# Down projection of a spectral layer with an FFN: each 512-column matmul issued as two of 256 columns

## The chip, the cores and the metric

The kernel runs on one core of one Trainium2 chip. The metric is the device time of one execution in microseconds, lower is better. Before the change it is 2627.49 us, the median of 3 runs (2627.15 to 2628.44).

On the core, TensorE multiplies matrices: a matmul streams the columns of its moving operand (`rhs`) past 128x128 weights (`lhsT`) and writes or adds into a bank of PSUM, 512 fp32 columns wide. The weights get there by a load that stands in front of each matmul as an instruction of its own. VectorE, ScalarE and GpSimd do the elementwise work, and SyncE issues the transfers.

## The reference

```
X = rfft(x, axis=1)                                  # x: 8 x 3008 x 256
Yr = X.real @ w_r - X.imag @ w_i + b_r
Yi = X.real @ w_i + X.imag @ w_r + b_i
Y = shrink(Yr, 0.01) + 1j * shrink(Yi, 0.01)         # sign(y) * max(|y| - 0.01, 0)
y = irfft(Y, n=3008, axis=1).reshape(24064, 256)
h = y @ w_in                                         # 256 -> 2048
g = h * clip(h + 3, 0, 6) / 6
out = g @ w_out                                      # 2048 -> 256, "down projection"
```

## The kernel before

**Precision.** A value is split into a high and a low part of type float32r, and a product is the sum of three matmuls: low x high, high x low, high x high (`product`, L137, and the two-letter keys of `STEPS` for the down projection).

**Stages.** The two Fourier transforms are small matmuls of 64, 47 and 128 points, with a trip through DRAM between them (L308, L394, L471, L523; their results go into the banks `ps_a`, and `pb` for the first sequence). For one sequence after the other they leave columns of `y`, 256 features by 512 tokens, in tiles `raw`. 47 such chunks of tokens go through the FFN in 8 steps each, so there are 376 units, each of 256 hidden features and 512 tokens.

**A unit.** The up projection of a unit is one Strassen-Winograd step: 7 blocks of 3 matmuls of 256 columns (weights `w_in`, moving operand `yb`, both hi and lo) into three banks: `pb` (two buffers; blocks 1, 6, 7 and 4 add up in it, and it is read by ScalarE between them, L585 and L619), `pc` (block 5, and then block 3 on top of it; VectorE reads it after each, L590) and `pd` (block 2; read by VectorE, L590). `pc` and `pd` have one buffer each. The sums stand in `h`. The gate is then four instructions of 1024 columns: ScalarE `r = relu(h + 3)` (L626), VectorE `r = min(r, 6) * h` (L628), ScalarE `gs` high (a cast, L130), VectorE `gs` low (L131).

**The down projection of a unit** (`down`, L649) is 12 matmuls of 512 columns in four steps of three: for two slices `u` of the hidden features and two halves `dh` of the 256 outputs, w_out low x g high, w_out high x g high, and w_out high x g low. They add up in two banks `po0` and `po1` over the 8 units of a chunk; after the last, ScalarE and VectorE copy the banks to `ot` (times 1/6), which is stored. That makes 376 x 12 = 4512 matmuls of this line.

**What sets the order.** The code lays a unit's phases one behind another (phase A of unit i, down step 0 of unit i - 3, phase C of unit i - 1, and so on), and hangs the pieces of the Fourier stages of the next sequences into slots between them. A planner then orders the instructions of each engine anew: it plays the program on a timeline with prices of its own, and picks at each point, by readiness and place in the code, what goes next (`TileContext(nc, schedule_with_timeline_sim=True)`). So a matmul that is priced or cut in another way can move every instruction behind it, on every engine.

Of the kernel before, what the change touches and what calls it, by code (L numbers as in the profile page):

```python
# [21 lines left out]
B, S, D, FF = 8, 3008, 256, 2048  # L22
# [3 lines left out]
P = 128  # L26
# [7 lines left out]
H = T // 2  # L34
# [66 lines left out]
def spectral_ffn(ctx: ExitStack, tc: tile.TileContext, x, w_r, w_i, bias, w_in, w_out, f47, f64, g64, sgn, out):  # L101
    nc = tc.nc
# [11 lines left out]
    def space(shape, dt, name, tag=None):  # L114
        tag = tag or name
        return sb.tile(shape, dt, name=name, tag=tag, bufs=depth.get(tag, 1))
# [41 lines left out]
    nf = NFT // 2  # L158
# [403 lines left out]
    def prepare(c):  # L562
        y = raw.pop(c)
        b11, b12, b21, b22 = y[:, 0, :H], y[:, 0, H:], y[:, 1, :H], y[:, 1, H:]
        s = space([P, 4, H], F32, "T")
        for to, p, q in ((0, b12, b11), (1, b22, s[:, 0]), (2, b22, b12), (3, b21, s[:, 1])):
            (nc.gpsimd if c else nc.vector).tensor_tensor(out=s[:, to], in0=p, in1=q, op=ALU.subtract)
        yield
        for n, src in ((2, b21), (1, b11), (6, s[:, 1]), (7, s[:, 2]), (5, s[:, 0]), (4, s[:, 3]), (3, b22)):
            t = space([P, 2, H], F32R, "yb")  # L570
            split(t[:, 0], t[:, 1], src, nc.gpsimd if c else nc.vector)
            yb[c, n] = (t[:, 0], t[:, 1])
            yield

    units = [(c, f) for c in range(NC) for f in range(nf)]
    hs, ps_of, keep, gs, pos = {}, {}, {}, {}, {}
# [63 lines left out]
    def down(i, step):  # L640

        c, f = units[i]
        g = gs[i]
        for u, dh, which, low in STEPS[step]:
            if f == 0 and step < 2 and u == 0 and which == "l":
                pos[dh] = ps_o.tile([P, 512], F32, name=f"po{dh}")
            ft = 2 * f + u
            w = wout_s["hl".index(which)]
            nc.tensor.matmul(  # L649
                out=pos[dh],  # L650
                lhsT=w[:, ft * D + dh * P : ft * D + (dh + 1) * P],
                rhs=g[:, low, u],
                start=f == 0 and u == 0 and which == "l",
                stop=f == nf - 1 and u == 1 and low == 1,
            )
            if f == nf - 1 and u == 1 and low == 1:
                ot = space([P, T], F32, "ot")
                if dh:
                    nc.vector.tensor_scalar(out=ot, in0=pos[dh], scalar1=1.0 / 6.0, scalar2=None, op0=ALU.mult)
                else:  # L660
                    nc.scalar.mul(out=ot, in_=pos[dh], mul=1.0 / 6.0)
                nc.sync.dma_start(out=out[dh * P : (dh + 1) * P, c * T : (c + 1) * T], in_=ot)
# [42 lines left out]
    for c in range(1, NC):  # L705
        g = prepare(c)
# [24 lines left out]
    for i in range(n + 3):  # L731
        for kind, f in ((in_band, i), (out_band, i - 3)):
            while 0 <= f < nf and (kind, f) not in ready:
                turn(LATE)
        if i < n:
            phase_a(i)
        gated(i - 2)
        fill(4 * i)
        if 0 <= i - 3 < n:
            down(i - 3, 0)  # L740
        if 0 <= i - 1 < n:
            phase_c(i - 1)
        fill(4 * i + 1)
        if 0 <= i - 3 < n:
            down(i - 3, 1)
        if i < n:
            phase_b(i)
        fill(4 * i + 2)
        if 0 <= i - 3 < n:
            down(i - 3, 2)  # L750
        if 0 <= i - 1 < n:
            phase_d(i - 1)
            gates[i - 1] = gate(i - 1)
            gated(i - 1)
        fill(4 * i + 3)
        if 0 <= i - 3 < n:
            down(i - 3, 3)
            gs.pop(i - 3)
# [47 lines left out]
```

## Time and profile before

| | us | share of the span |
|---|---|---|
| median of 3 runs | 2627.49 | |
| span of the profiled execution | 2628.8 | 100% |
| TensorE matmuls busy | 2554.0 | 97% |
| TensorE weight loads busy | 2278.1 | 87% |
| VectorE busy | 1967.7 | 75% |
| ScalarE busy | 1816.7 | 69% |
| GpSimd busy | 762.9 | 29% |

The profiled execution's own time is its span, 2628.8 us, which is 0.4 us above the slowest of the three timed runs. Matmuls are pipelined, and their ends are modelled: a 512-column matmul is shown with 396 ns, though the next one starts 233 ns after it. So the busy time of a matmul is not its price. Its price is the distance from its start to the next start where nothing waits, and rows that merge several issues give it (duration by number). In the listings, PE is the matmul, PEld the weight load, DVE is VectorE, ACT ScalarE, POOL GpSimd, SP SyncE.

### The profile page before, as it was taken

To read this page: it belongs to the slowest core of one execution; us is meant where nothing else is said; L and a number is where in the kernel's file an instruction comes from. 1 tells how busy PE (TensorE), PEld (TensorE's weight loads), DVE (VectorE), ACT (ScalarE), POOL (GpSimd) and SP (SyncE) were. 2 spreads that over 40 slices of the span, in tenths; PEclk is the share of its full clock that TensorE was granted. 3 is DMA by queue.
4 is the path that set the end of the run, shared out by engine and by line. 5 is a ranking of instruction groups with operands and counts; after the bars stand their busy time and mean duration, and the time that the engine had idled before them with its cause. 6 is when DMAs were issued, how large, how long until landed. Compare 5 with 4: busy or idle time off the path is not lost.

```text
span 2628.8 us, 44438 instructions
## 1 busy us (share of the span) xinstructions
PE 2554.0 (97%) x16392; PEld 2278.1 (87%) x16392; DVE 1967.7 (75%) x3195; ACT 1816.7 (69%) x3578; POOL 762.9 (29%) x726
## 2 busy tenths in 40 slices
PE   5789999999999999999999999999999999999999
PEld 4568989988898988998898888898989889888887
DVE  7777877777777777777778777787777777666766
ACT  5467776767677676676766677766776766776666
POOL 3223333333323332333314243233321121131310
PEclk8999999999999999999999999999999999999999
DMA  8643422232123212322223222222222111110000
GB/s 245 204 127 91 121 83 79 82 89 69 56 85 90 76 58 64 86 86 82 62 66 91 75 65 74 74 81 80 66 76 64 44 60 50 40 31 25 12 17 17
DMA packets 150081, 199.97 MB, mean 76 GB/s; under 512 B 16847, under 2 KB 103943, under 8 KB 149863
## 3 DMA queue, kind: packets, MB, share of 16 engines
q1 hardware_dynamic: 149863, 197.13, 25.7%
q8 instruction: 129, 2.11, 0.4%
q14 instruction: 89, 0.73, 0.1%
HBM read 97.45 MB, written 74.97 MB: 66 GB/s over the span
## 4 chain that ended last, share of the span: by engine, by line
PE 83%; DVE 6%; ACT 5%; DMA 4%; issue 1%; SPq 0%; POOL 0%; ACTq 0%; DVEq 0%
PE po L649 37%; PE pb L137 17%; PE ps_a L137 10%; PE pc L137 9%; PE pd L137 4%; PE ps_a L523 3%; PE ps_a L394 2%; ACT r L626 2%; DVE r L628 1%; ACT gs L130 1%; DMA scr<-a 1%; DMA xin<-in_x 1%; DVE gs L131 1%; DVE h L590 1%; DMA zt<-tc 1%
## 5 line engine op out<-in xcount | busy, mean ns | idle before, releaser
L649 PE MATMUL po<-gs,w_out_hi 128*128 128x512 f32 x3008 | 1008.5, 396 | 0.0
L628 DVE SCALAR_TENSOR_TENSOR r<-r,h 128x1024 f32<-128x1024 f32 x376 | 485.2, 1290 | 253.0 <-ACT r L626 250.9
L649 PEld LDWEIGHTS po<-gs,w_out_hi 128*128 128x128 f32 x3008 | 540.6, 188 | 83.7
L649 PE MATMUL po<-gs,w_out_lo 128*128 128x512 f32 x1504 | 602.9, 401 | 5.3 <-ACT gs L130 3.2
L137 PE MATMUL pb<-yb,w_in_hi 128*128 128x256 f32 x3008 | 570.1, 279 | 0.0
L626 ACT ACTIVATE r<-h,three 128x1024 f32<-128x1024 f32 x376 | 435.6, 1158 | 193.8 <-DVE h L590 191.1
L131 DVE TENSOR_TENSOR gs<-r,gs 128x1024 fp32r<-128x1024 f32 x376 | 481.9, 1282 | 75.6 <-ACT gs L130 74.1
L137 PEld LDWEIGHTS pb<-yb,w_in_hi 128*128 128x128 f32 x3008 | 459.1, 188 | 18.2
L130 ACT CAST gs<-r 128x1024 fp32r<-128x1024 f32 x376 | 396.7, 1055 | 97.3 <-DVE r L628 94.5
L590 DVE TENSOR_TENSOR h<-pc,u 128x256 f32<-128x256 f32 x752 | 315.3, 419 | 183.7 <-PE pc L137 168.4
L131 POOL TENSOR_TENSOR yb<-T,yb 128x256 fp32r<-128x256 f32 x184 | 176.7, 966 | 908.5 <-ACT yb L130 905.3
L137 PE MATMUL pb<-yb,w_in_lo 128*128 128x256 f32 x1504 | 430.5, 287 | 3.8 <-ACT p L585 0.9
L585 ACT COPY u<-pb 128x256 f32<-128x256 f32 x752 | 279.4, 374 | 112.6 <-PE pb L137 93.8
L649 PEld LDWEIGHTS po<-gs,w_out_lo 128*128 128x128 f32 x1504 | 282.7, 188 | 63.8 <-ACT gs L130 14.3
L137 PEld LDWEIGHTS pb<-yb,w_in_lo 128*128 128x128 f32 x1504 | 282.6, 188 | 28.2 <-ACT h L619 4.0
L137 PE MATMUL pc<-yb,w_in_hi 128*128 128x256 f32 x1504 | 296.8, 279 | 0.0
L137 PEld LDWEIGHTS pc<-yb,w_in_hi 128*128 128x128 f32 x1504 | 229.8, 188 | 11.7
L137 PE MATMUL pc<-yb,w_in_lo 128*128 128x256 f32 x752 | 217.7, 289 | 2.0 <-DVE h L590 1.7
L585 ACT COPY p<-pb 128x256 f32<-128x256 f32 x376 | 140.3, 374 | 71.6 <-PE pb L137 70.5
L619 ACT COPY h<-pb 128x256 f32<-128x256 f32 x376 | 141.2, 376 | 53.0 <-PE pb L137 51.7
L590 DVE TENSOR_TENSOR h<-pd,p 128x256 f32<-128x256 f32 x376 | 157.0, 418 | 19.8 <-ACT p L585 13.5
L137 PEld LDWEIGHTS pc<-yb,w_in_lo 128*128 128x128 f32 x752 | 141.6, 188 | 16.4 <-DVE h L590 3.9
(139 smaller groups left out, 3873.7 us busy)
## 6 DMA issues: line engine op xcount, KB each, us to landing
bt<-scr SPq DMA_DIRECT2D x96, 256.0 KB, 3.0
scr<-pt SPq DMA_DIRECT2D x96, 256.0 KB, 2.3
zt<-tc SPq DMA_DIRECT2D x376, 64.0 KB, 2.0
out<-ot SPq DMA_DIRECT2D x94, 256.0 KB, 2.3
scr<-a SPq DMA_DIRECT2D x96, 240.0 KB, 2.6
qt<-scr SPq DMA_DIRECT2D x96, 240.0 KB, 3.5
xin<-in_x SPq DMA_DIRECT2D x42, 480.0 KB, 4.6
f<-in_f SPq DMA_DIRECT2D x96, 128.0 KB, 2.7
```

The source lines that it names most:

```text
L130: nc.scalar.copy(out=hi, in_=src)
L131: (on or nc.vector).tensor_tensor(out=lo, in0=src, in1=hi.bitcast(F32), op=ALU.subtract)
L137: nc.tensor.matmul(out=ps, lhsT=a, rhs=b, start=start and n == 0, stop=stop and n == len(todo) - 1, skip_group_check=more,)
L394: nc.tensor.matmul(out=psv[:, dh, :, u, :], lhsT=data[:, u, dh * P : (dh + 1) * P], rhs=f[:, u, :], start=True, stop=True,)
L523: nc.tensor.matmul(out=ps[:, cs * w + g * rows : cs * w + (g + 1) * rows], lhsT=qt[:rows, cs, g, dh * P : (dh + 1) * P], rhs=f47_s[2][:row ...
L585: nc.scalar.copy(out=t, in_=ps)
L590: nc.vector.tensor_tensor(out=to, in0=ps, in1=keep.pop((i, n)), op=ALU.add)
L619: nc.scalar.copy(out=hs[i][:, 1, :H], in_=pb)
L626: nc.scalar.activation(out=r, in_=h, func=AF.Relu, bias=three, scale=1.0)
L628: nc.vector.scalar_tensor_tensor(out=r, in0=r, scalar=6.0, in1=h, op0=ALU.min, op1=ALU.mult)
L649: nc.tensor.matmul(out=pos[dh], lhsT=w[:, ft * D + dh * P : ft * D + (dh + 1) * P], rhs=g[:, low, u], start=f == 0 and u == 0 and which == ...
```

## The change

Each matmul of the down projection is issued as two: the same weights, the first and the second 256 columns of the moving operand, into the first and the second half of the same bank. Nothing else in the code changes; `H` is 256.

```
-            nc.tensor.matmul(
-                out=pos[dh],
-                lhsT=w[:, ft * D + dh * P : ft * D + (dh + 1) * P],
-                rhs=g[:, low, u],
-                start=f == 0 and u == 0 and which == "l",
-                stop=f == nf - 1 and u == 1 and low == 1,
-            )
+            for half in range(2):
+                cols = slice(half * H, (half + 1) * H)
+                nc.tensor.matmul(
+                    out=pos[dh][:, cols],
+                    lhsT=w[:, ft * D + dh * P : ft * D + (dh + 1) * P],
+                    rhs=g[:, low, u, cols],
+                    start=f == 0 and u == 0 and which == "l",
+                    stop=f == nf - 1 and u == 1 and low == 1,
+                    skip_group_check=True,
+                )
```

The planner deals with 4512 more matmuls, and the order changes on all engines from the first down projection on. Two places on TensorE show how. The first is the bank `pc` of the 64th unit: its block 5, what stands behind it, and its block 3, which must wait until VectorE has read block 5. Before (`pc_6694`):

```order
L137 MATMUL pc_6694<-yb_5834,w_in_lo_79 128x256 [waits DVE_49]
L137 MATMUL pc_6694<-yb_5834,w_in_hi_78 128x256 x2
L137 MATMUL pb_6666<-yb_6439,w_in_lo_79 128x256 [waits Activation_49]
L137 MATMUL pb_6666<-yb_6439,w_in_hi_78 128x256 [waits Pool_49]
L137 MATMUL pb_6666<-yb_6439,w_in_hi_78 128x256
L137 MATMUL pb_6772<-yb_6373,w_in_lo_79 128x256 [waits Activation_49]
L137 MATMUL pb_6772<-yb_6373,w_in_hi_78 128x256 x2
L137 MATMUL pc_6694<-yb_5933,w_in_lo_79 128x256 [waits DVE_49]
L137 MATMUL pc_6694<-yb_5933,w_in_hi_78 128x256 x2
```

And now (`pc_7429` is the same unit's bank), from the last two matmuls of block 5 on:

```order
L137 MATMUL pc_7429<-yb_6440,w_in_hi_78 128x256 x2
L651 MATMUL po1_6986<-gs_7335,w_out_hi_226 128x256 x2
L651 MATMUL po0_6981<-gs_7335,w_out_hi_226 128x256 x2
L651 MATMUL po1_6986<-gs_7335,w_out_hi_226 128x256 x2
L523 MATMUL ps_a_7565<-f47_all_88,qt_7365 128x120 [waits PE_49]
L523 MATMUL ps_a_7565<-f47_all_88,qt_7365 128x120 x3
L137 MATMUL pb_7322<-yb_6487,w_in_lo_79 128x256 [waits Activation_49]
L137 MATMUL pb_7322<-yb_6487,w_in_hi_78 128x256 x2
L137 MATMUL pb_7398<-yb_7094,w_in_lo_79 128x256 [waits Activation_49]
L137 MATMUL pb_7398<-yb_7094,w_in_hi_78 128x256 [waits Pool_49]
L137 MATMUL pb_7398<-yb_7094,w_in_hi_78 128x256
L137 MATMUL pc_7429<-yb_6551,w_in_lo_79 128x256 [waits DVE_49]
```

Between the two blocks stood 6 matmuls of 256 columns; now there are 12 of them and 4 of 120 columns. The second place is the start of the 162nd unit's down projection, which must wait for the gate of that unit (`gs_14535` before, `gs_16455` now; `gs_14466` and `gs_16374` are the unit before it). Before:

```order
L649 MATMUL po1_14546<-gs_14466,w_out_hi_226 128x512
L137 MATMUL pd_14595<-yb_13940,w_in_lo_79 128x256 [waits DVE_49]
L137 MATMUL pd_14595<-yb_13940,w_in_hi_78 128x256 x2
L394 MATMUL ps_a_14725<-f64_14117,bt_14116 128x2x64
L137 MATMUL ps_a_14797<-xs_14687,f47_lo_87 120x512 [waits PE_49]
L137 MATMUL ps_a_14797<-xs_14687,f47_hi_86 120x512 [waits Pool_49]
L137 MATMUL ps_a_14797<-xs_14687,f47_hi_86 120x512
L137 MATMUL pc_14548<-yb_14095,w_in_lo_79 128x256 [waits DVE_49]
L137 MATMUL pc_14548<-yb_14095,w_in_hi_78 128x256 x2
```

And now, from the middle of the down projection before it, whose halves are no longer side by side at one place:

```order
L651 MATMUL po0_16463<-gs_16374,w_out_hi_226 128x256 [waits DVE_49]
L137 MATMUL pc_16471<-yb_15949,w_in_lo_79 128x256 [waits DVE_49]
L137 MATMUL pc_16471<-yb_15949,w_in_hi_78 128x256 x2
L651 MATMUL po0_16463<-gs_16374,w_out_hi_226 128x256
L137 MATMUL pb_16361<-yb_16007,w_in_lo_79 128x256 [waits Activation_49]
L137 MATMUL pb_16361<-yb_16007,w_in_hi_78 128x256 x2
L651 MATMUL po1_16468<-gs_16374,w_out_hi_226 128x256 x2
L651 MATMUL po0_16463<-gs_16374,w_out_hi_226 128x256 x2
L651 MATMUL po1_16468<-gs_16374,w_out_hi_226 128x256 x2
L137 MATMUL ps_a_16756<-xs_16628,f47_lo_87 120x512 [waits PE_49]
```

Before, the down projection of the unit before ended ahead of `pd`, and two more blocks into `pb` followed the rows shown, then the first matmul from `gs_14535`. Now another block and another product stand between. Counted from the last matmul that feeds the unit's `h` to the first that reads its `gs`, there were 17 matmuls of 256 columns, 7 of 512 and 3 of 128; now there are 39 of 256, 6 of 512 and 4 of 128.

## Rows read from the trace of the kernel before

**Rows 1.** The page, busy time and instructions of each engine.

```profile
PE 2554.0 (97%) x16392; PEld 2278.1 (87%) x16392; DVE 1967.7 (75%) x3195; ACT 1816.7 (69%) x3578; POOL 762.9 (29%) x726
```

**Rows 2.** The page, the chain that ended last, by engine and by line.

```profile
PE 83%; DVE 6%; ACT 5%; DMA 4%; issue 1%; SPq 0%; POOL 0%; ACTq 0%; DVEq 0%
PE po L649 37%; PE pb L137 17%; PE ps_a L137 10%; PE pc L137 9%; PE pd L137 4%; PE ps_a L523 3%; PE ps_a L394 2%; ACT r L626 2%; DVE r L628 1%; ACT gs L130 1%; DMA scr<-a 1%; DMA xin<-in_x 1%; DVE gs L131 1%; DVE h L590 1%; DMA zt<-tc 1%
```

**Rows 3.** Windows of the span: stretch, length, busy times, clock, DMA share, GB/s.

```profile
0.00:100.00 100.00, 67.00 (x389) 52.64 (x390) 75.97 (x127) 55.50 (x103) 29.50 (x34) 0.93 0.73 221
100.00:200.00 100.00, 78.59 (x422) 57.89 (x421) 75.84 (x141) 61.77 (x130) 29.84 (x34) 0.90 0.54 158
...
1200.00:1600.00 400.00, 396.48 (x2562) 355.77 (x2561) 304.14 (x499) 281.95 (x561) 135.97 (x119) 1.00 0.26 76
```

**Rows 4.** TensorE by line and shape: count | busy, mean ns | idle before.

```profile
L649 PE MATMUL po<-gs,w_out_hi 128*128 128x512 f32 x3008 | 1008.5, 396 | 0.0
L649 PE MATMUL po<-gs,w_out_lo 128*128 128x512 f32 x1504 | 602.9, 401 | 5.3 <-ACT gs L130 3.2
```

**Rows 5.** The chain from 700 to 740 us: start, duration, what, merged issues.

```profile
703.32 1.86 PE po L649 x8
705.18 0.71 PE pb L137 x6
705.89 0.93 PE po L649 x4
706.81 0.35 PE pc L137 x3
...
713.84 0.89 PE ps_a L394 x8
714.73 1.87 PE po L649 x8
...
733.54 0.69 PE pb L137 x6
734.23 1.86 PE po L649 x8
```

**Rows 6.** The chain from 1000 to 1030 us.

```profile
1018.09 0.68 PE pb L137 x6
1018.77 1.86 PE po L649 x8
```

**Rows 7.** Waits of weight loads from 200 us on: total, times, longest.

```profile
PEld po L649 <- ACT gs L130: 14.3, 44, 1.3
PEld pb L137 <- ACT h L619: 3.8, 14, 0.3
PEld pc L137 <- DVE h L590: 3.2, 9, 0.6
PEld pb L137 <- ACT p L585: 3.1, 7, 0.9
PEld pd L137 <- DVE h L590: 3.0, 4, 1.2
```

**Rows 8.** Timeline of TensorE at the 64th unit's `pc`: start, duration, what.

```profile
606.14 0.39 PE L137 MATMUL pb<-yb,w_in_hi 128*128 128x256 f32 x2
606.36 0.38 PE L137 MATMUL pc<-yb,w_in_lo 128*128 128x256 f32 x1
606.59 0.40 PE L137 MATMUL pc<-yb,w_in_hi 128*128 128x256 f32 x2
606.82 0.41 PE L394 MATMUL ps_a<-f,bt 128*128 128x128 f32 x2
```

**Rows 9.** Timeline of TensorE at the 162nd unit's down projection.

```profile
1274.66 0.39 PE L137 MATMUL pb<-yb,w_in_hi 128*128 128x256 f32 x2
1275.22 0.50 PE L649 MATMUL po<-gs,w_out_lo 128*128 128x512 f32 x1 [0.17 <-ACT gs L130]
1275.56 0.40 PE L649 MATMUL po<-gs,w_out_hi 128*128 128x512 f32 x1
1275.79 0.39 PE L649 MATMUL po<-gs,w_out_lo 128*128 128x512 f32 x1
```

## The prediction

> **What bounds the kernel now.** I read the busy line first: TensorE's matmuls are busy for 97% of the span, its weight loads for 87%, VectorE for 75% [rows 1]. The counts there already say something about the change: there are as many weight loads as matmuls, 16392 each, although in every product two of the three matmuls use the same high weights one after the other. A load is issued with every matmul, needed or not, so the change adds 4512 matmuls and 4512 loads.
>
> Next the chain of waits: 83% of the span is TensorE's own, one matmul behind another, and the down projection at L649 is the largest piece with 37% [rows 2]. Then the stretches: the first 200 us are another regime (67 and 79 us of 100 busy, clock 0.93 and 0.90, DMA share 0.73 and 0.54), and in the middle TensorE is busy for 396 of 400 us at a full clock [rows 3]. The change first moves an instruction at the first down projection, so what lies ahead of it stays as it is. Behind it the time is a sum over matmuls, each with the distance to the next start, plus what TensorE waits.
>
> Busy means can't be used as that price: 396 and 401 ns are shown for a 512-column matmul [rows 4], yet 8 of them take 1.86 us [rows 5].
>
> **The change part by part.**
>
> First the stream. It removes 4512 issues of 512 columns (3008 and 1504) [rows 4] and adds 9024 of 256. The trace has both shapes, with the same type, the same load in front of each, and the same kind of accumulation into one bank. For 512 columns the pieces of the chain give 1.86/8 = 232.5 ns, 0.93/4 = 232.5 and 1.87/8 = 233.8 [rows 5]. For 256 they give 0.71/6 = 118.3, 0.35/3 = 116.7, 0.69/6 = 115.0 [rows 5] and 0.68/6 = 113.3 [rows 6]. A pair of halves so costs between 226.7 and 236.7 ns in place of 232.5 to 233.8. That is between -7.1 and +4.2 ns per issue, times 4512: -32 to +19 us. The two inner rows, 115.0 and 116.7, give pairs of 230 and 233.3, which hold the old price between them and within 2.5 ns. I take the stream at 0, because these rows stand all along the span and the ends are each one kind of stretch.
>
> The added load costs nothing as long as it hides under a matmul. It had 232 ns of cover and now has some 115. How near is that to its limit? 8 matmuls of 128 columns with a load each take 0.89 us, 111 ns each [rows 5]: a quarter of the columns, but hardly less time than 256. So a pair of load and matmul does not go below 111 ns here, and a half is only 2 to 7 ns above that. This cover is thin; it is the third rival below.
>
> Then the order. 4512 more instructions make the planner lay all engines anew, and what TensorE waits is set by how much other work stands between a result and its use. I counted that over the whole order before and after, each matmul between at its spacing (116, 233 and 111 ns). At the 64th unit the second block into `pc` came 6 matmuls = 0.70 us behind the first, and now comes 12 and 4 = 1.8 us behind it. In the trace the short distance costs: the second matmul of the block starts 0.23 us behind the first instead of 0.115, since its load was late too [rows 8]. Over all 376 units there are 22 such distances under 0.9 us before, and 6 after. For successive blocks in one `pb`, distances under 0.7 us fall from 35 to 14, and for a new `pd` those under 1.2 us from 5 to 2. The largest wait is the gate's. At the 162nd unit, 17, 7 and 3 matmuls between the last sum and the first use of `gs` were 3.9 us; now 39, 6 and 4 are 6.4 us. The trace shows 0.56 us where two matmuls of 256 should take 0.23, so 0.33 lost, and then 0.34 instead of 0.23 for the first issue [rows 9]. Distances under 4.5 us fall from 39 to 12.
>
> The prices: a load's wait on the gate is 14.3/44 = 0.33 us, on `pb` (3.8 + 3.1)/21 = 0.33, on `pc` 3.2/9 = 0.36, on `pd` 3.0/4 = 0.75 [rows 7], and each is followed by a late second matmul at 0.11 [rows 8, 9]. If every short distance that goes were a full wait, 27 x 0.44 + 21 x 0.44 + 16 x 0.47 + 3 x 0.86 = 31 us would go. That is the upper end. At the other end nothing goes, or waits come in places that the counts don't see (the order of VectorE, ScalarE and the transfers moved as well); I bound it by +10 us, a third of the upper end with its sign turned. Short distances and waits do not match one to one (35 against 21 waits for `pb`, 22 against 9 for `pc`), so I take a third of the upper end: -10 us.
>
> What else is added hides: more instructions to fetch and issue lie beside a stream that already ran at 113 to 118 ns per issue. VectorE, ScalarE and the copies to `ot` get the same instructions; their banks are complete when the second half of the last matmul is, as now. Nothing is late next in place of a wait that goes: behind it stands the next matmul.
>
> The sum is 0 - 10 = -10 us. The profiled execution is 2628.8 us long, 1.3 above the median; the difference is put on the median: 2627.5 - 10 = 2617.5, say 2618 us.
>
> **The rivals.** A difference of 0.2% (5.3 us) is about what a measurement of this kernel can tell from none, so "faster" is below 2622.2 and "slower" above 2632.7.
>
> *The halves are quicker than I take them.* If they run as in the best stretch, 226.7 ns a pair against 232.5 [rows 5, 6], the stream gives 5.8 x 4512 = 26 us: 2601 with no change of the waits. For it: the two halves use the same weights and nothing moves between them. Against: the two high matmuls of every product do that too, and are in all the rows above.
>
> *The time does not change.* The waits that go come back elsewhere: a gate that is reached later by TensorE is also produced later, if ScalarE and VectorE work in another order. Then the stream at 0 leaves 2627. For it: 83% of the chain is matmuls, and they keep their columns. Against: the distances grow for all four kinds at once.
>
> *Each issue has a price of its own, and the time grows.* The place is TensorE's stream, the mechanism the load's cover: where the load and matmul pair needs 118 ns, as in 0.71/6 [rows 5], a half can't be faster, and the pair is 236.7 ns. That is +4.2 x 4512 = +19 us, 2637 with the waits' gain and 2646 without. It decides from 118 ns per half on: 5.3 us over the time before, with the waits' 10 us taken off, is 15.3 us of stream or 3.4 ns per pair, on top of 232.5 to 233.8. Without the waits' gain 117 ns are enough. For it: these 118-ns stretches are long (from 700 to 730 us), and the floor of 111 is near. Against: 115 and 116.7 stand beside them. The Trainium skill has a rule on this side too: by its page "TensorE: Matmul & The Clock Gate", section "Wait — 56ns, not 53.3ns?", a matmul at the full clock takes its columns plus about 2.5 ns that do not depend on their number. By that rule the change would cost an estimated 4512 x 2.5 = 11 us, 2639 us. The trace doesn't show such a part: two issues of 256 take no longer than one of 512 in its middle rows.
>
> **How the numbers follow.** The forecast, fewer waits at an equal stream, has 0.42; the quicker halves 0.13; no change 0.27; the price per issue 0.18. So faster is 0.42 + 0.13 = 0.55, same 0.27, slower 0.18. The range leaves out most of the full gain of the first rival together with the waits' (2591) and the worst of the third (2646): 2602 to 2637.
>
> **What the profile after would show.** Pieces of the down projection in the chain with 0.115 to 0.117 us per issue; the span's share of the chain by TensorE as now or a little higher; waits of loads on `gs` below 44 and 14.3 us, on `pb` and `pc` about half. If halves show 118 ns or more all along, the third rival holds. If they show 116 and the waits total what they did, the second does. I am wrong altogether if weight loads come in other numbers than matmuls, or if the clock falls in the steady stretch.

## The result: 37 us faster, and the profile after

The changed kernel takes 2590.66 us (median of 4 runs, 2589.71 to 2591.84) against 2627.6 beside it: a ratio of 0.9853, 95% interval 0.9842 to 0.9865. The forecast was 2618, its range ended at 2602; the time lies 11 us below that.

The page of after, busy times and the chain, columns as in [rows 1, 2]:

```profile
PE 2521.4 (97%) x20904; PEld 2459.9 (95%) x20904; DVE 1965.3 (76%) x3195; ACT 1820.9 (70%) x3578; POOL 754.8 (29%) x726
...
PE 87%; DVE 5%; ACT 3%; DMA 3%; issue 1%; POOL 0%; SPq 0%; ACTq 0%; DVEq 0%; POOLq 0%
```

Loads and matmuls are still equal in number, 4512 more of each. TensorE's own share of the chain rose from 83% to 87% of a shorter span [rows 2]: 13% of 2589.6 us is left to the others instead of 17% of 2628.8, about 110 us less. These shares are rounded, and where an engine stands in the chain its time is not all TensorE's wait, so this shows the direction and not the size.

Two questions are left: what does a half cost, and what became of the waits? First the half, in pieces of the chain of after (start, duration, what, merged issues), from 700 to 740 us and from 1000 to 1030 us:

```profile
701.57 0.68 PE pb L137 x6
702.25 0.91 PE po L651 x8
...
713.87 0.91 PE po L651 x8
...
1016.66 1.89 PE po L651 x16
1018.55 0.71 PE pb L137 x6
```

0.91/8 = 113.8 ns and 1.89/16 = 118.1 ns: the halves show the two levels of the up projection's matmuls beside them, 0.68/6 = 113.3 and 0.71/6 = 118.3, as before [rows 5, 6]. A pair is 227.6 to 236.2 ns in place of 232.5 to 233.8.

Then the waits of weight loads from 200 us on (total, times, longest), as in [rows 7]:

```profile
PEld po L651 <- ACT gs L130: 6.7, 22, 0.8
PEld pc L137 <- DVE h L590: 1.9, 4, 0.8
...
PEld pd L137 <- DVE h L590: 1.0, 3, 0.4
...
PEld pb L137 <- ACT u L585: 0.9, 3, 0.3
PEld pb L137 <- ACT p L585: 0.8, 2, 0.5
...
PEld pb L137 <- ACT h L619: 0.6, 2, 0.4
```

The gate's wait fell from 14.3 us in 44 waits to 6.7 in 22, `pd` from 3.0 to 1.0, `pc` from 3.2 to 1.9, and the wait of `pb` for ScalarE's `h` from 3.8 us in 14 waits to 0.6 in 2. The place of [rows 9], the 162nd unit's down projection, in TensorE's timeline of after:

```profile
1258.53 0.63 PE L137 MATMUL ps_a<-z,g_hi 128*128 128x512 f32 x2
1259.00 0.40 PE L651 MATMUL po<-gs,w_out_lo 128*128 128x256 f32 x2
1259.24 0.40 PE L651 MATMUL po<-gs,w_out_hi 128*128 128x256 f32 x2
```

Two matmuls of 512 columns, 0.47 us to the first half, and 0.24 for its pair: nothing is lost here, where 0.33 and 0.11 us were.

### The profile page after: what moved, and what is told of

The parts are those of the page before. It is cut to its first block, busy times and chain, and to the rows that moved or that the text cites. A ratio compares the mean times of both kernels' runs of the same rounds, so it can differ in the third digit from the quotient of the medians.

```text
span 2589.6 us, 53384 instructions
## 1 busy us (share of the span) xinstructions
PE 2521.4 (97%) x20904; PEld 2459.9 (95%) x20904; DVE 1965.3 (76%) x3195; ACT 1820.9 (70%) x3578; POOL 754.8 (29%) x726
## 4 chain that ended last, share of the span: by engine, by line
PE 87%; DVE 5%; ACT 3%; DMA 3%; issue 1%; POOL 0%; SPq 0%; ACTq 0%; DVEq 0%; POOLq 0%
PE po L651 37%; PE pb L137 18%; PE ps_a L137 11%; PE pc L137 9%; PE pd L137 5%; PE ps_a L523 3%; PE ps_a L394 3%; ACT gs L130 1%; DVE r L628 1%; ACT r L626 1%; DMA xin<-in_x 1%; DMA zt<-tc 1%; DMA scr<-a 1%; DMA qt<-scr 0%; DVE gs L131 0%
## 5 line engine op out<-in xcount | busy, mean ns | idle before, releaser
L651 PE MATMUL po<-gs,w_out_hi 128*128 128x256 f32 x6016 | 1034.1, 278 | 0.0
L651 PEld LDWEIGHTS po<-gs,w_out_hi 128*128 128x128 f32 x6016 | 846.2, 188 | 1.5
L651 PE MATMUL po<-gs,w_out_lo 128*128 128x256 f32 x3008 | 608.1, 280 | 2.3 <-ACT gs L130 1.0
L651 PEld LDWEIGHTS po<-gs,w_out_lo 128*128 128x128 f32 x3008 | 462.4, 188 | 8.8 <-ACT gs L130 6.7
L137 PE MATMUL pd<-yb,w_in_hi 128*128 128x256 f32 x752 | 149.7, 279 | 0.0
```

Source lines behind the costliest of these rows:

```text
L137: nc.tensor.matmul(out=ps, lhsT=a, rhs=b, start=start and n == 0, stop=stop and n == len(todo) - 1, skip_group_check=more,)
L651: nc.tensor.matmul(out=pos[dh][:, cols], lhsT=w[:, ft * D + dh * P : ft * D + (dh + 1) * P], rhs=g[:, low, u, cols], start=f == 0 and u == ...
```

## The experiments

**The order and the issue, each alone.** The change does two things: it issues halves, and it makes the planner lay all engines anew. A kernel was written that builds the program twice. The first build plans it with the matmul cut in `ORDER_OF` pieces; the order of every engine is read off. The second build issues it as `ISSUED_AS` pieces, and ties every instruction behind its predecessor in that order, without any wait. The edit is shown against the changed kernel and cut at the dots; `PIECES` holds the slices of each cut, and the first runs call it `HALVES`. These kernels are some lines longer, so L649 of before is L656 or L668 in their listings:

```
-            for half in range(2):
-                cols = slice(half * H, (half + 1) * H)
+            for cols in PIECES[cut[0]]:
...
+        cut[0] = pieces
+        with tile.TileContext(nc, schedule_with_timeline_sim=True, name="spectral_ffn") as tc:
+            spectral_ffn(tc, **args)
...
+                for key in like:
+                    for n in keys[key]:
+                        i = by_name[n]
+                        if i.engine in last:
+                            tc.add_manual_dep(i, last[i.engine], ...NoSync...)
+                        last[i.engine] = n
...
+    _, order = build(ORDER_OF)
+    nc, _ = build(ISSUED_AS, order)
```

Halves in the order of before (`ORDER_OF, ISSUED_AS = 1, 2`):

> Halves, each pair side by side at the place that the whole matmul has before; every engine in the order of before. Theory A (two causes: the stream of the 4512 issues is about 2.5 ns per pair and 11 to 16 us in all cheaper, the new order takes away some 23 us of TensorE's waits): the stream's part alone, 2612 to 2617 us. Rival B (all of the gain is the halves themselves, the order is no matter): about 2591. Rival C (all of it is the order): 2625 to 2630.

Measured: 2624.18 us against 2630.15, ratio 0.9977 (0.9968 to 0.9987), so -6 us. Rival B falls. Theory A had -11 to -16, and gets half of it. Rival C, which gives the halves nothing, misses by less: 2624.18 lies just below its 2625, and the interval ends below 1. The waits hardly moved, as the loads of this kernel show:

```profile
PEld po L656 <- ACT gs L134: 14.3, 44, 1.2
PEld pd L141 <- DVE h L594: 4.1, 7, 1.2
PEld pb L141 <- ACT h L623: 3.6, 13, 0.3
```

Whole matmuls in the new order (`2, 1`):

> Whole matmuls of 512 columns, each at the place that its first half has after the change; every engine in the order of after. Theory A: the order's part alone, 2603 to 2607 us, with the waits of weight loads as few as after. Rival B (the halves alone): 2627. Rival C (the order alone): 2591. Rival D (the finer order pays only when halves are really issued, since a whole matmul holds TensorE twice as long where a half fits): 2615 to 2627.

Measured: 2601.76, ratio 0.9892 (0.9878 to 0.9905), so -28 us without a single half issued. Rivals B and D fall, and so does C, which wanted all of the gain (2591); theory A's order part (2603 to 2607) is missed by 1 us. The chain from 1000 to 1030 us shows the whole matmul at its old price, 1.86/8 = 232.5 ns, and the waits of loads are those of after:

```profile
1014.23 1.86 PE po L656 x8
1016.09 0.69 PE pb L141 x6
```

```profile
PEld po L656 <- ACT gs L134: 6.3, 20, 0.9
PEld pc L141 <- DVE h L594: 1.7, 4, 0.8
PEld pb L141 <- ACT h L623: 1.2, 2, 0.9
PEld pb L141 <- ACT p L589: 1.0, 2, 0.8
...
PEld pd L141 <- DVE h L594: 0.6, 2, 0.4
```

Both together, the parted halves put side by side (`2, 2`):

> The change, with the halves that the planner had parted (other matmuls between them) put together at the place of the first; every engine otherwise in the order of after. Theory A: as after, 2589 to 2593 us. If the parted halves matter by themselves (rival D), 2595 or more.

Measured: 2590.74, ratio 0.985 (0.9837 to 0.9864): the time of after. That the planner parts some pairs is worth nothing by itself. On one baseline the table reads: order -28, halves -6, both -39. The two sum to -34; the 5 us more when they stand together are about the size of the intervals (each some 3 us wide to a side). So the order is worth 28 us with whole matmuls and 33 with halves, and the halves 6 in the old order and 11 in the new.

The traces of these runs show both parts in every distance from one matmul's start to the next, from the first down projection on. A distance counts as late above 243 ns for 512 columns and above 126 for fewer, and its lateness is what it has over 233 ns (512 columns), 117 (256) or 110 (fewer). The lateness adds up to 70 us before, 72 with halves in the old order, 43 with whole matmuls in the new order and 47 after. So the 28 us of the order are time that TensorE waited. The distances of the down projection that are not late have means of 232.6 ns for the whole and 115.5 for a half in the old order, and 232.3 and 115.0 in the new, so a pair of halves is about 2 ns quicker. All engines were moved together here, so these runs do not tell which engine's order brings the 28 us.

**Would any other order do?** Before, with the two output banks named in the other sequence:

```
-        ((0, 0, "l", 0), (0, 0, "h", 0), (0, 1, "l", 0)),
-        ((0, 1, "h", 0), (1, 0, "l", 0), (1, 0, "h", 0)),
+        ((0, 1, "l", 0), (0, 1, "h", 0), (0, 0, "l", 0)),
+        ((0, 0, "h", 0), (1, 1, "l", 0), (1, 1, "h", 0)),
...
```

> Before, with the two output banks of the down projection named in the other sequence in the table of steps, so that the planner lays the same work of 512 columns in another order. Theory A (whole matmuls leave the planner no finer place, so the counts of short distances stay: 22 for the second block of a pc before and 22 here, 35 and 39 for successive blocks of a pb): 2622 to 2632 us. Rival E (the old order was merely unlucky, any other is as good as the new): 2605 to 2612.

Measured: 2630.03, ratio 0.9997 (0.9987 to 1.0006). Rival E falls: this one other order with whole matmuls is like the old.

**Are more short distances away still better?** Halves, in the order planned with quarters (`4, 2`):

> Issued as halves, in the order that the planner makes when the down projection is cut in quarters of 128 columns (every half at the place of its first quarter, all engines in that order). Counted over the order, short distances almost vanish: second block of a pc under 0.9 us 22 before, 6 after the change, 1 here; successive blocks of a pb under 0.7 us 35, 14, 4; gate under 4.5 us 39, 12, 1. Theory A (TensorE's waits follow these distances): the steady waits, some 69 us before and 45 after, fall again by 10 to 20 us, so 2570 to 2580 us. Rival F (beyond the new order more distance buys nothing, or is paid elsewhere: other engines and transfers late): 2588 to 2600.

Measured: 2772.06, ratio 1.0547 (1.0533 to 1.0562). Both fail: rival F had other engines late, but no later than 2600. The order with the fewest short distances on TensorE is the slowest of all with halves. Its gate waits are nearly gone, as counted, and the loads wait elsewhere:

```profile
PEld pc L153 <- DVE h L606: 86.4, 163, 1.5
PEld pb L153 <- ACT u L601: 49.5, 89, 1.4
...
PEld po L668 <- ACT gs L146: 2.0, 1, 2.0
```

One such place, in VectorE's timeline and then in TensorE's (start, duration, engine, line, what):

```profile
1301.83 1.07 DVE L147 TENSOR_TENSOR z<-zt,z 128x512 fp32r<-128x512 f32 x1
1302.83 0.41 DVE L606 TENSOR_TENSOR h<-pd,p 128x256 f32<-128x256 f32 x1
1303.37 1.23 DVE L147 TENSOR_TENSOR gs<-r,gs 128x1024 fp32r<-128x1024 f32 x1
1304.51 0.41 DVE L606 TENSOR_TENSOR h<-pc,u 128x256 f32<-128x256 f32 x1
```

```profile
1304.11 0.63 PE L668 MATMUL po<-gs,w_out_hi 128*128 128x256 f32 x4
1304.98 0.39 PE L153 MATMUL pc<-yb,w_in_lo 128*128 128x256 f32 x1 [0.24 <-DVE h L606]
```

The 0.41 us read of `pc` stands in VectorE's queue behind a 1.23 us piece of the gate, so TensorE, whose next block into `pc` starts only when that read has ended, comes 0.4 us late (0.87 us for four halves). The distance on TensorE is long, but the place in the other queue is bad. The same order for TensorE alone, with the other engines laid anew by the planner for halves:

```
+                        if i.engine != mybir.EngineType.PE:
+                            continue
```

> Halves; only TensorE keeps the order of the plan with quarters (the one that gave 2772 us), VectorE, ScalarE, GpSimd and the queue are laid anew by the planner, which now sees halves. Theory H (the 2772 came from VectorE's and ScalarE's queues, where the small reads of pc and pb that TensorE waits for were laid behind 1.2 us instructions of the gate, on a plan that took TensorE for slower): the 86 us of loads waiting for VectorE's h and some 70 us for ScalarE's u, p and h mostly go, 2575 to 2600 us. Rival I (TensorE's own order with its long distances is what is bad): 2700 or more.

Measured: 2605.04, ratio 0.9905 (0.989 to 0.992). In the traces TensorE's sequence is the same as in the run before. Of the 143 us over before all go and 25 more; the time lies 5 us above the expected range, and 18.8 us of the waits on `pc` are left:

```profile
PEld pc L153 <- DVE h L606: 18.8, 33, 1.4
```

Rival I falls. What the 2772 came from is the order that VectorE, ScalarE, GpSimd and the queue had with this order of TensorE.

**Which plan gives a good order?** Three more plans, the first issued whole (496 and 16 columns in the plan), the others as halves (384 and 128; thirds):

> Whole matmuls, in the order that the planner makes when each is cut into 496 and 16 columns: two issues to plan, but no finer place for most of the columns. Counts: second block of a pc 5 (22 before), blocks of a pb 29 (35), gate under 4.5 us 45 (39). Theory A (each wait belongs to its kind of distance): the waits on pc go, the gate's stay or grow, 2617 to 2627 us. Rival G (it is enough that the planner has two issues per matmul and takes TensorE for slower): as the whole matmuls in the new order, 2600 to 2606.

Measured: 2676.97, ratio 1.0184 (1.017 to 1.0198). Both expectations fail. The gate's waits grew to 25.5 us, more than the count of short distances (45 against 39) says, `pd` waits 15.6 us, and `pc` waits 15.0 us where it waited 3.2 before, though its short distances fell from 22 to 5:

```profile
PEld po L668 <- ACT gs L146: 25.5, 50, 2.6
PEld pd L153 <- DVE h L606: 15.6, 36, 1.2
PEld pc L153 <- DVE h L606: 15.0, 22, 2.7
```

> Halves, all engines in the order that the planner makes when each matmul is cut into 384 and 128 columns: as many issues to plan as with halves, but cut unevenly. If the good order comes from what two issues per matmul do to the plan's clock and grain, as after: 2586 to 2600 us (short distances 4, 12 and 9 against 6, 14 and 12). If the even cut matters, more than 2610.

Measured: 2604.55, ratio 0.9903 (0.9888 to 0.9918): between the two cases. An uneven cut brings 25 of the 39 us, with fewer short distances than after.

> Halves, all engines in the order planned for three issues per matmul (192, 192 and 128 columns). Theory H (the plan's TensorE gets slower with each issue that is not there on the chip): between two issues (2591) and four (2772), 2640 to 2720 us, the waits on VectorE's reads of pc and ScalarE's of pb as with quarters but fewer. If the long distances were good by themselves: below 2590.

Measured: 2619.72, ratio 0.9958 (0.9941 to 0.9974). The sign of theory H is right, worse than two issues and better than four, the size is missed: it is still better than before. The waits on `pc` came as expected, fewer than with quarters but far more than after:

```profile
PEld pc L153 <- DVE h L606: 16.4, 33, 1.5
```

**Where cutting ends.** Quarters of 128 columns, issued at the places of before (`1, 4`):

> Four issues of 128 columns in the place of each whole matmul, all engines in the order of before. If a pair of weight load and matmul cannot go below some 97 to 111 ns, as the 128-column matmuls of the transforms show, a whole matmul's 233 ns become 390 to 444 and the time 3340 to 3580 us. If the time goes by columns alone, as from one issue to two, it stays at 2615 to 2630.

Measured: 3575.13 in one run. The chain from 1000 to 1030 us gives the price:

```profile
1001.58 3.52 PE po L668 x32
...
1014.82 3.52 PE po L668 x32
```

3.52/32 = 110 ns for 128 columns, so 440 per whole matmul: 4512 x (440 - 232.5) = 936 us, of 946 measured. So from 256 columns to 128 a pair of load and matmul goes only from about 115 ns to 110: 256 columns are just above what looks like a floor. Whether the load or the matmul sets it, no run separates.

**A version with all of it.** The other 468 float32r matmuls of 512 columns as halves too, planned and issued so:

```
+        pieces = [slice(0, H), slice(H, T)] if wide == T else [slice(0, wide)]
         for n, (a, b) in enumerate(todo):
-            nc.tensor.matmul(out=ps, lhsT=a, rhs=b, ...)
+            for k, cols in enumerate(pieces):
+                nc.tensor.matmul(out=ps[:, cols], lhsT=a, rhs=b[:, cols], ...)
```

> The change, and the 468 other float32r matmuls of 512 columns (transforms of the later sequences) issued as halves as well, with the order that the planner makes of it. Theory A: 468 x 2.5 ns = 1.2 us from the stream, and the short distances as after (4, 15 and 8 against 6, 14 and 12): 2584 to 2592 us, the same as after within what can be measured.

Measured: 2586.74, ratio 0.9842 (0.9828 to 0.9855). It is the fastest of all, but its interval overlaps that of after (0.9842 to 0.9865), so it is not told apart from it.

## Why the prediction was wrong

The direction held, and most of the gain sits where the forecast put it, in TensorE's waits. The rivals "the time does not change" and "each issue has a price of its own" are out, the latter with its 2637 to 2646 us. What failed is the size of both terms, and the count of distances that the first was read from.

*"I take a third of the upper end: -10 us."* This is the step that failed. The order alone brought -28 us with whole matmuls and -33 with halves, about the whole upper end of 31. The third was chosen because short distances and listed waits did not match one to one, but that says nothing of the size. With whole matmuls in the new order the five kinds of [rows 7] fell from 27.4 us in 78 waits to 10.8 in 30. At 0.11 us for the late second matmul behind each, that is 16.6 + 5.3 = 22 us; in the distances from start to start the whole 28 us show.

*"I take the stream at 0."* Inside its bounds (-32 to +19), but mis-sized: -6 us in the old order, or 1.3 ns per pair, and 11 us between whole and halves in the new one, or 2.4 ns per pair. The two inner rows gave 230 and 233.3 for a pair; 230 was the better one. So the first rival, the quicker halves, held in part: it had 26 us.

*"The distances grow for all four kinds at once"*, brought against the second rival, was true and pointed the right way, but it is no measure. The plan with quarters left the fewest short ones, and its order cost 143 us; the plan with 496 and 16 columns had far fewer for `pc`, and `pc` waited longer. The count looked at TensorE's order only. Which instruction stands ahead in VectorE's and ScalarE's queues can decide as much, and I had left this with "the order of VectorE, ScalarE and the transfers moved as well". So even the direction was in part luck: the same count made me expect a gain for the slowest kernel with halves.

*"More instructions to fetch and issue lie beside a stream"* held: the 400 us from 1200 us on hold 3335 matmuls where 2562 were, and TensorE is busy in 398 of them (columns as in [rows 3]):

```profile
1200.00:1600.00 400.00, 398.13 (x3335) 392.34 (x3335) 308.19 (x503) 286.59 (x567) 123.01 (x116) 1.00 0.27 76
```

*The range.* It left out most of the case in which the first rival and the waits' gain come together (2591). The time fell there, but by another sum: 28 to 33 us of order and 6 to 11 of stream, not 10 and 26.

Shown is so: 28 to 33 of the 37 to 39 us are the order, which the planner made when it saw two halves, and most of that is time that TensorE waited (27 us less lateness with whole matmuls, 25 with halves). Not settled is why this order is the good one. One other order of whole matmuls (swapped banks) brought nothing, more pieces (thirds, quarters) brought less or cost time, and two pieces are not enough: 496 and 16 columns cost 48 us. That the planner's own prices for TensorE come nearest to the chip's with two halves is a guess; they were not varied by themselves.

## What to carry to other kernels

Where a planner orders the program, a change of one instruction's shape is two changes, and each can be run alone by taking the order from one build and the instructions from another: here the order brought three to five times what the shape did. A count of distances on one engine sees half of it: ask for each wait also what is queued ahead of the releasing instruction on its own engine. And a matmul with a load of its own can be cut for free only until the pair of load and matmul reaches its floor: here 256 columns gained a little, and 128 cost 946 us.

## What the runs showed of the hardware

Float32r matmuls with a load each take 232.5 to 233.8 ns for 512 columns, 113 to 118 for 256, and 110 for 128. So the price goes by columns down to 256 and is nearly flat from there to 128, and two halves are a little cheaper than the whole, which I had given a small chance: 0.2% of the kernel in an unchanged order, with a 95% interval (0.9968 to 0.9987) that ends below 1. Two halves with the same weights one behind the other still have a load each: the page of after has 20904 of either.
